# A new written-out order for a fused retention and channel-mix kernel

## The chip, the cores and the metric

The kernel runs on one core of one Trainium2 chip. The metric is the device time of one execution in microseconds. The core has five engines with queues of their own: TensorE (PE, with its weight loads shown apart as PEld), VectorE (DVE), ScalarE (ACT), GpSimd (POOL) and SyncE (SP, which only issues DMAs here). Each engine works its own list in order and waits for the others through semaphores. Sixteen DMA engines move the data.

## The reference

The inputs q, k and v have the shape batch 4, heads 8, time 768, width 64. The first half is a recurrent attention with a decay gamma for each head; the second half is a channel mix on its result, with 512 channels and 1024 hidden ones:

```python
for t in range(S):
    state = gamma * state + einsum('bhd,bhe->bhde', k[:, :, t], v[:, :, t])
    y[:, :, t] = scale * einsum('bhd,bhde->bhe', q[:, :, t], state)
x = y.transpose(0, 2, 1, 3).reshape(B, S, H * D)
x_prev = x shifted by one step in time, zero at the start
xk = mu_k * x + (1 - mu_k) * x_prev
xr = mu_r * x + (1 - mu_r) * x_prev
k = relu(xk @ w_k)
out = sigmoid(xr @ w_r) * (k * k @ w_v)
```

## The kernel before

The sequence of each batch is cut into three blocks of 256 steps, so there are 12 blocks, 0 to 11; a state is carried through the three blocks of one batch. Within a block the recurrence is done as matrix products: masked scores inside two chunks of 128 steps (u = 0 and 1), and a state T32 or TG that is decayed from chunk to chunk.

The whole program is one long list of words, the text ORDER at line 16, written out by hand or by a planner; the loop at the end of the kernel takes word after word and calls the function of its code. A word's code is what is done, its first number the block, and the numbers behind @ are the banks of the accumulator memory (PSUM, eight banks, 0 to 7) that it writes. The order of the words is the order of each engine's list. Tiles are used in rings, so a piece also waits until the last reader of its ring slot is done: four slots for q, k and v each, three for scaled keys, turned q and k, masked scores, mixed inputs and hidden values, two for differences, five for gates and results.

| code | line | engine | what |
|---|---|---|---|
| lq, lv, wk, wv, wr | 176, 511, 518, 514 | GpSimd's DMA queue | load q, v (cast to 16 bits), halves of w_k and w_v, w_r |
| lk | 176 | SyncE's queue, or GpSimd's where its third place is 2 | load k |
| ks | 189 | VectorE (last number 0) or GpSimd (1) | scale the keys by their decay |
| T, Tq, Tk | 204, 222 | TensorE | turn keys or q (T in 128 x 128 pieces, Tq and Tk in 64 x 64) |
| E | 250 | ScalarE | copy turned q (0) or k (1) from PSUM |
| S, M | 258, 265 | TensorE, VectorE | scores; mask them |
| C, U, G | 283, 295 or 299, 302 | TensorE, VectorE, GpSimd | state of a block; add; decay |
| I, Y, D | 314, 327, 341 | TensorE, TensorE, VectorE | output from the state; from the masked scores; to xT |
| Du, du, Xu, Ku, Qu | 349, 356, 370, 387, 395 | | block 0's D, dx, X, K and Q in halves of 128 steps |
| dx, X | 356, 370 | VectorE or GpSimd; VectorE | difference to the step before; mixed inputs, four slices for each of xk (0) and xr (1) |
| K, Q | 407, 414 and 417 | TensorE, ScalarE | a quarter of the hidden layer; relu and square |
| R, s | 421, 427 | TensorE, ScalarE | gate product; sigmoid |
| V, O, st | 433, 439, 446 | TensorE, VectorE, SyncE's queue | value product in two parts; result; store |
| Vc, Oc, sc | 451, 458, 466 | | the last half block's V, O and st in two halves |
| z | 495 | TensorE | zero matmuls, as many as the number says |
| mu, mt, me | 483, 488, 491 | ScalarE's queue, TensorE, ScalarE | load mu; turn it; copy it |
| gy | 501, 504 | VectorE | powers of the decay |

A word such as `lq.0.0.2` loads only the slices 0 to 2 of four: block 0's q and k come in halves. `Ku.0.1.0` is the second half of the hidden layer (1) for the first 128 steps (0) and reads the second half of w_k, `wk.1`. `V.n.tb.0` reads `wv.0` and the first half of the hidden values, `V.n.tb.1` the rest.

Two places of the code matter for the steps. A load's queue is chosen by the word, and a bank or ring slot is what ties pieces together beyond their data:

```python
def load_k(n, e=0, j0=0, j1=NJ):
    load((nc.sync, nc.scalar, nc.gpsimd)[e], k, K32, n, j0, j1)
def store(n, tb):
    nc.sync.dma_start(out=out[b, t0 : t0 + P, :], in_=OS(2 * n + tb))
```

Of the kernel before, what the change touches and what calls it, by code (L numbers as in the profile page):

```python
# [25 lines left out]
V.0.0.0@7 R.0.1@2 R.0.0@0 V.0.1.1 D.1 dx.1.0 X.1.0.1.2 X.1.0.2.3 X.1.0.3.4 X.1.0.0.1 s.0.0 s.0.1
X.1.1.0.1 O.0.1 X.1.1.1.2 ks.2.0 X.1.1.2.3 X.1.1.3.4 K.1.3@0 lq.4 lv.3 lq.5 Q.1.3 K.1.0@2 K.1.2@6
Tq.2@01 Q.1.0 E.2.0 C.2@2 T.2.1@4 E.2.1 V.0.0.1 R.1.0@0 Q.1.2 lv.5 U.1.1 G.1.1 U.2.0 G.2.0 ks.3.1
ks.4.1 O.0.0 S.2.0@45 M.2.0 I.2.0@67 S.2.1@23 K.1.1@1 R.1.1@4 T.3.1@5 s.1.0 Q.1.1 ks.5.1 M.2.1 Y.2
D.2 dx.2.0 Tq.3@23 V.1.1.0@1 V.1.1.1 T.4.1@0 T.5.1@6 V.1.0.0@7 E.3.0 s.1.1 E.3.1 E.4.1 O.1.1  # L30
S.3.0@01 Tq.4@45 V.1.0.1 E.5.1 E.4.0 X.2.0.1.2 X.2.0.2.3 M.3.0 X.2.0.0.1 X.2.0.3.4 C.3@23 S.4.0@45
Tq.5@01 U.3.0 X.2.1.2.3 X.2.1.0.1 U.3.1 M.4.0 E.5.0 K.2.2@6 K.2.1@2 K.2.3@3 Q.2.2 Q.2.1 I.3.0@45
S.3.1@01 lv.4 lk.6.2 lk.7.2 lq.6 G.3.1 lv.6 lq.7 X.2.1.1.2 X.2.1.3.4 M.3.1 O.1.0 ks.6.0 K.2.0@2
R.2.1@6 Q.2.3 Q.2.0 s.2.1 Y.3 S.5.0@23 C.4@01 D.3 V.2.1.0@6 T.6.1@7 R.2.0@4 V.2.1.1 V.2.0.0@5
V.2.0.1 E.6.1 s.2.0 lk.10 st.0.0 dx.3.1 M.5.0 X.3.0.0.1 X.3.0.2.3 X.3.0.1.2 X.3.0.3.4 X.3.1.2.3
K.3.1@4 K.3.0@7 U.4.0 G.4.0 O.2.0 U.4.1 O.2.1 ks.7.1 G.4.1 Q.3.1 Q.3.0 I.4.0@45 Tq.6@01 S.4.1@23
K.3.2@6 K.3.3@7 M.4.1 X.3.1.0.1 X.3.1.3.4 X.3.1.1.2 C.5@2 Y.4 U.5.0 st.1.0 lk.9 st.2.0 lk.11
# [538 lines left out]
```

## Time and profile before

| what | value |
|---|---|
| median of 3 runs | 160.04 us (159.6, 160.04, 162.05) |
| the profiled execution | 160.76 us |
| its span, first to last instruction | 158.7 us |
| busy: PE, DVE, ACT, POOL | 149.2, 123.6, 93.8, 63.4 us |
| read from and written to memory | 24.25 MB, 6.29 MB |
| first half of q, v, second half of q of block 0 landed | 6.65, 8.09, 8.81 us |
| v, k and q of block 1 landed | 11.28, 12.81, 14.08 us |
| wk.0, wk.1, wv.0, wr, wv.1 landed | 16.60, 19.13, 21.69, 24.23, 26.77 us |
| q, k and v of block 2, k of block 3 landed | 28.27, 30.15, 31.30, 33.14 us |
| first Ku, first V, Y.4 started | 18.20, 23.42, 61.33 us |

The profile is one execution. Its page gives the busy time of each engine, a chain that leads from the last instruction back to what released each step, and groups of instructions by line. Times count from the start of the span; the execution's own time is 2.1 us longer than its span. Landings are the times at which the trace shows a load complete. A busy PE is one with a matmul under way, and its ends are modelled. Steps between the starts of pieces are used where pieces overlap a little.

### The profile page before, as it was taken

How to read it: one execution, taken by the hardware profiler on the slowest of the kernel's cores; microseconds unless marked ns; L12 is line 12 of the kernel's file. 1: busy time of each engine (PE TensorE's matmuls, PEld its weight loads, DVE VectorE, ACT ScalarE, POOL GpSimd, SP SyncE). 2: the span in 40 equal slices, each digit the busy share in tenths (PEclk: the TensorE clock that was granted, in tenths of full speed). 3: DMA queues.
4: the chain of work that ended last, by engine and by line, in shares of the span. 5: the costliest groups of instructions: out<-in, count | busy, mean ns of one | idle time of the engine just before them, and what ended most of it. 6: DMA issues, size and time to landing. Idle time of an engine off the chain costs nothing.

```text
span 158.7 us, 5766 instructions
## 1 busy us (share of the span) xinstructions
PE 149.2 (94%) x2564; PEld 96.6 (61%) x2564; DVE 123.6 (78%) x217; ACT 93.8 (59%) x149; POOL 63.4 (40%) x69
## 2 busy tenths in 40 slices
PE   6977899899998999998999999999999999999991
PEld 2344683766585577575667576576486585675760
DVE  2568899776998789999969789975997887992321
ACT  3230665775977349467667675277665556276950
POOL 7937593589932457703013306291014114000000
PEclk9999999999999999999999999999999999999999
DMA  5999999999999986999408910712050050001242
GB/s 149 168 243 207 208 206 246 281 260 185 136 287 164 235 268 163 290 179 131 45 10 321 126 14 4 68 46 95 0 202 0 0 202 4 0 0 66 82 172 80
DMA packets 36872, 21.99 MB, mean 139 GB/s; under 512 B 25832, under 2 KB 32880, under 8 KB 36848
## 3 DMA queue, kind: packets, MB, share of 16 engines
q0 software_dynamic: 28768, 13.11, 59.2%
q1 hardware_dynamic: 7632, 8.26, 15.3%
q8 instruction: 20, 0.33, 0.8%
q10 hardware_dynamic: 448, 0.26, 0.6%
q14 instruction: 4, 0.03, 0.1%
HBM read 24.25 MB, written 6.29 MB: 192 GB/s over the span
## 4 chain that ended last, share of the span: by engine, by line
PE 79%; DMA 10%; DVE 4%; POOL 2%; issue 2%; DVEq 0%; POOLq 0%
PE ps L433 24%; PE ps L407 23%; PE ps L421 12%; DMA k<-in_k_dram 7%; PE ps L258 4%; DMA q<-in_q_dram 4%; PE ps L327 4%; PE ps L314 3%; PE ps L222 3%; PE ps L283 2%; PE ps L204 2%; POOL q L176 1%; PE ps L451 1%; DVE xk L370 1%; PE ps L495 1%
## 5 line engine op out<-in xcount | busy, mean ns | idle before, releaser
L433 PE MATMUL ps<-wv,k 128*128 128x512 f16 x184 | 44.9, 380 | 0.0
L407 PE MATMUL ps<-xk,wk 128*128 128x256 f16 x352 | 43.2, 273 | 0.0
L414 ACT ACTIVATE kr<-ps 128x512 f32<-128x512 f32 x44 | 26.0, 591 | 21.9 <-PE ps L407 21.9
L407 PEld LDWEIGHTS <-wk 128*128 128x128 f16 x352 | 33.2, 98 | 8.1 <-DVE xk L370 0.7
L265 DVE TENSOR_TENSOR a<-ps,c_sb 128x1024 f16<-128x1024 f32 (+1 forms) x26 | 29.2, 1137 | 2.3 <-PE ps L258 2.3
L417 ACT ACTIVATE k<-kr 128x512 f16<-128x512 f32 x44 | 27.7, 630 | 1.4
L433 PEld LDWEIGHTS <-k 128*128 128x128 f16 x184 | 17.1, 98 | 18.3 <-ACT k L417 1.0
L302 POOL TENSOR_TENSOR tg<-t,csm_sb 128x256 f16<-128x256 f32 x16 | 9.8, 610 | 43.9 <-DVE t L299 43.9
L421 PE MATMUL ps<-wr,xr 128*128 128x512 f16 x96 | 24.4, 379 | 0.7 <-issue 0.7
L439 DVE SCALAR_TENSOR_TENSOR os<-ps,rs 128x512 f32<-128x512 f32 x23 | 15.5, 686 | 11.6 <-ACT rs L427 8.4
L370 DVE SCALAR_TENSOR_TENSOR xk<-dx,mu,xT 128x256 f16<-128x256 f32 (+1 forms) x52 | 21.4, 459 | 2.9 <-POOL dx L356 2.7
L370 DVE SCALAR_TENSOR_TENSOR xr<-dx,mu,xT 128x256 f16<-128x256 f32 (+1 forms) x52 | 21.9, 459 | 0.0
L427 ACT ACTIVATE rs<-ps 128x512 f32<-128x512 f32 x24 | 13.8, 592 | 12.1 <-PE ps L421 12.1
L250 ACT COPY kT<-ps 128x1024 f16<-128x1024 f16 (+1 forms) x13 | 12.1, 953 | 11.1 <-PE ps L204 7.7
L341 DVE TENSOR_TENSOR xT<-ps,gy_sb 128x1024 f32<-128x1024 f32 x11 | 13.4, 1223 | 5.3 <-PE ps L327 3.8
L250 ACT COPY qT<-ps 128x1024 f16<-128x1024 f16 (+1 forms) x13 | 12.2, 940 | 8.6 <-PE ps L222 7.8
L421 PEld LDWEIGHTS <-xr 128*128 128x128 f16 x96 | 8.9, 98 | 10.3 <-issue 1.1
L176 POOL DMA_DIRECT2D v<-in_v_dram x12 | 10.8, 904 | 10.3 <-PE ps L327 4.7
L189 POOL TENSOR_TENSOR ks<-k,csm_sb 128x1024 f16<-128x1024 f32 x7 | 13.2, 1899 | 2.5 <-DMA k<-in_k_dram 2.5
L176 POOL DMA_DIRECT2D q<-in_q_dram x13 | 11.7, 898 | 3.3 <-PE ps L421 1.6
L258 PE MATMUL ps<-qT,kT 64*64 64x128 f16 x384 | 11.9, 220 | 1.1 <-ACT qT L250 0.7
L356 POOL TENSOR_TENSOR dx<-xT 128x1024 f32<-128x1024 f32 x4 | 7.6, 1891 | 9.1 <-DVE xT L341 9.1
(45 smaller groups left out, 144.5 us busy)
## 6 DMA issues: line engine op xcount, KB each, us to landing
out_dram<-os SPq DMA_DIRECT2D x23, 256.0 KB, 2.6
k<-in_k_dram POOLq DMA_DIRECT2D x8, 512.0 KB, 9.4
v<-in_v_dram POOLq DMA_DIRECT2D x12, 256.0 KB, 6.1
q<-in_q_dram POOLq DMA_DIRECT2D x11, 256.0 KB, 8.3
k<-in_k_dram SPq DMA_DIRECT2D x3, 512.0 KB, 5.2
wk<-in_moe_w_k_dram POOLq DMA_DIRECT2D x2, 512.0 KB, 11.1
wv<-in_moe_w_v_dram POOLq DMA_DIRECT2D x2, 512.0 KB, 12.5
k<-in_k_dram SPq DMA_DIRECT2D x2, 256.0 KB, 3.6
```

The costliest lines, as they stand in the source:

```text
L176: eng.dma_start(out=d(n)[:, 2 * j0 : 2 * j1], in_=rows(x, n)[:, 2 * j0 : 2 * j1])
L250: nc.scalar.copy(out=out, in_=pt)
L258: nc.tensor.matmul(pa[u * D : u * D + D, hp, j, :], lhsT=KT(n)[r, j, i, u * D : u * D + D], rhs=QT(n)[r, j, u, :], start=(j == j0), stop=( ...
L265: nc.vector.tensor_tensor(out=A2(n)[:, i, :, j0:j1], in0=pairs(banks("S", n, i, j0))[:, :, j0:j1], in1=causal[:, i, None, None, :].to_broa ...
L370: nc.vector.scalar_tensor_tensor(out=XM[w](n)[:, j, t0:t1], in0=DX(n)[:, j, t0:t1], scalar=mu[:, w * NCO + j : w * NCO + j + 1], in1=x[:, ...
L407: nc.tensor.matmul(pz[:, i, :], lhsT=wk16[:, co, fo * P : fo * P + P], rhs=XM[0](n)[:, co, :], start=(i == 0 and co == 0), stop=(co == NCO ...
L414: nc.scalar.activation(out=kr, in_=banks("K", n, g).rearrange("p (i t) -> p i t", i=2), func=AF.Relu)
L417: nc.scalar.activation(out=K2(n)[:, 2 * g : 2 * g + 2], in_=kr, func=AF.Square)
L421: nc.tensor.matmul(banks("R", n, tb), lhsT=XM[1](n)[:, co, tb * P : tb * P + P], rhs=wr16[:, co, :], start=(co == 0), stop=(co == NCO - 1),)
L427: nc.scalar.activation(out=RS(2 * n + tb), in_=banks("R", n, tb), func=AF.Sigmoid, scale=1.0 / KSC)
L433: nc.tensor.matmul(banks("V", n, tb, 0), lhsT=K2(n)[:, fo, tb * P : tb * P + P], rhs=wv16[:, fo, :], start=(fo == 0), stop=(fo == NFO - 1),)
L439: nc.vector.scalar_tensor_tensor(out=OS(2 * n + tb), in0=banks("V", n, tb, 0), scalar=1.0 / (KSC * KSC), in1=RS(2 * n + tb), op0=ALU.mult, ...
```

## The change

Only the text ORDER is changed. The same pieces of work are put in another order, with these differences in kind:

- v of block 0 is loaded ahead of both halves of q; v of block 1 comes behind wk.1, wk.1 ahead of wk.0, and k and q of block 2 ahead of wr, wv.0 and wv.1.
- k of block 10 goes to GpSimd's queue; blocks 9 and 11 stay on SyncE's, among other stores.
- The keys of blocks 1, 3, 4 and 5 are scaled on VectorE instead of GpSimd, those of 2, 6, 8 and 9 on GpSimd instead of VectorE.
- The differences of blocks 3, 7, 9 and 10 are on VectorE instead of GpSimd, those of 4, 5, 6 and 8 on GpSimd instead of VectorE.
- The keys of blocks 5 and 9 are turned in 64 x 64 pieces and those of 8 in 128 x 128; before, 8 was in 64 x 64 pieces and 5 and 9 were not.
- There are 24 zero matmuls instead of 27, and the load of mu is issued behind the first copy of ScalarE.
- Many banks are given out anew.

```diff
-lk.0.0.2.4 lk.0.0.0.2 lq.0.0.2 lv.0 lq.0.2.4 lv.1 lk.1.2 mu gy ks.0.0.2.4 ks.0.0.0.2 z.13@2
-Tq.0.0.2@01 lq.1 wk.0 wk.1 T.0.1.0.2@2 T.0.1.2.4@3 E.0.0.0.2 E.0.1.0.2 z.2@4 C.0@01 U.0.0 U.0.1
-wv.0 G.0.1 ks.1.1 wr wv.1 Tq.0.2.4@45 S.0.0.0.2@67 E.0.0.2.4 E.0.1.2.4 z.2@2 I.0.0@45 S.0.1.0.2@01
-S.0.0.2.4@23 M.0.0.0.2 M.0.0.2.4 mt@6 M.0.1.0.2 z.1@7 S.0.1.2.4@23 M.0.1.2.4 z.3@7 Y.0 z.2@7
-C.1@23 Du.0.0 Du.0.1 me T.1.1@4 Tq.1@01 E.1.1 E.1.0 z.4@7 S.1.0@01 du.0.0.0 du.0.0.1 Xu.0.0.0.2.3
-Xu.0.0.1.2.3 Xu.0.0.1.3.4 Xu.0.0.1.1.2 Xu.0.0.1.0.1 Ku.0.0.1@4 Xu.0.0.0.1.2 U.1.0 G.1.0 lq.2
-lk.2.2 M.1.0 Xu.0.1.0.2.3 Xu.0.0.0.3.4 Xu.0.0.0.0.1 Ku.0.1.1@2 Qu.0.0.1 lv.2 I.1.0@45 S.1.1@01
-lk.3.2 lk.4.2 lq.3 lk.5.2 Ku.0.1.0@6 Ku.0.0.0@7 Qu.0.1.0 Qu.0.0.0 Qu.0.1.1 Xu.0.1.0.1.2
-Xu.0.1.1.1.2 M.1.1 Y.1 Xu.0.1.0.3.4 Xu.0.1.1.2.3 Xu.0.1.1.3.4 Xu.0.1.0.0.1 Xu.0.1.1.0.1 V.0.1.0@6
-V.0.0.0@7 R.0.1@2 R.0.0@0 V.0.1.1 D.1 dx.1.0 X.1.0.1.2 X.1.0.2.3 X.1.0.3.4 X.1.0.0.1 s.0.0 s.0.1
-X.1.1.0.1 O.0.1 X.1.1.1.2 ks.2.0 X.1.1.2.3 X.1.1.3.4 K.1.3@0 lq.4 lv.3 lq.5 Q.1.3 K.1.0@2 K.1.2@6
-Tq.2@01 Q.1.0 E.2.0 C.2@2 T.2.1@4 E.2.1 V.0.0.1 R.1.0@0 Q.1.2 lv.5 U.1.1 G.1.1 U.2.0 G.2.0 ks.3.1
-ks.4.1 O.0.0 S.2.0@45 M.2.0 I.2.0@67 S.2.1@23 K.1.1@1 R.1.1@4 T.3.1@5 s.1.0 Q.1.1 ks.5.1 M.2.1 Y.2
-D.2 dx.2.0 Tq.3@23 V.1.1.0@1 V.1.1.1 T.4.1@0 T.5.1@6 V.1.0.0@7 E.3.0 s.1.1 E.3.1 E.4.1 O.1.1
-S.3.0@01 Tq.4@45 V.1.0.1 E.5.1 E.4.0 X.2.0.1.2 X.2.0.2.3 M.3.0 X.2.0.0.1 X.2.0.3.4 C.3@23 S.4.0@45
-Tq.5@01 U.3.0 X.2.1.2.3 X.2.1.0.1 U.3.1 M.4.0 E.5.0 K.2.2@6 K.2.1@2 K.2.3@3 Q.2.2 Q.2.1 I.3.0@45
-S.3.1@01 lv.4 lk.6.2 lk.7.2 lq.6 G.3.1 lv.6 lq.7 X.2.1.1.2 X.2.1.3.4 M.3.1 O.1.0 ks.6.0 K.2.0@2
-R.2.1@6 Q.2.3 Q.2.0 s.2.1 Y.3 S.5.0@23 C.4@01 D.3 V.2.1.0@6 T.6.1@7 R.2.0@4 V.2.1.1 V.2.0.0@5
-V.2.0.1 E.6.1 s.2.0 lk.10 st.0.0 dx.3.1 M.5.0 X.3.0.0.1 X.3.0.2.3 X.3.0.1.2 X.3.0.3.4 X.3.1.2.3
-K.3.1@4 K.3.0@7 U.4.0 G.4.0 O.2.0 U.4.1 O.2.1 ks.7.1 G.4.1 Q.3.1 Q.3.0 I.4.0@45 Tq.6@01 S.4.1@23
-K.3.2@6 K.3.3@7 M.4.1 X.3.1.0.1 X.3.1.3.4 X.3.1.1.2 C.5@2 Y.4 U.5.0 st.1.0 lk.9 st.2.0 lk.11
-st.0.1 st.1.1 lk.8.2 G.5.0 lq.8 Q.3.2 E.6.0 Q.3.3 V.3.1.0@6 R.3.1@0 V.3.1.1 s.3.1 D.4 dx.4.0
...
-Q.11.0 K.11.2@5 Q.11.2 K.11.3@1 O.9.0 X.11.1.0.1 Q.11.3 V.11.0.0@0 R.11.0@5 V.11.0.1 R.11.1@1
-Vc.11.1.0@4 Vc.11.1.1@6 s.11.0 st.8.1 st.7.1 st.8.0 O.10.1 O.10.0 st.9.0 st.10.1 st.10.0 st.9.1
-O.11.0 st.11.0 s.11.1 Oc.11.1.0 Oc.11.1.1 sc.11.1.0.0 sc.11.1.1.1
+lk.0.0.2.4 lk.0.0.0.2 lv.0 lq.0.0.2 lq.0.2.4 gy lk.1.2 lq.1 ks.0.0.2.4 wk.1 lv.1 ks.0.0.0.2 z.12@1
+T.0.1.0.2@0 T.0.1.2.4@1 E.0.1.0.2 mu z.5@4 Tq.0.0.2@23 C.0@45 E.0.0.0.2 Tq.0.2.4@67 U.0.0
+E.0.0.2.4 S.0.0.0.2@23 U.0.1 E.0.1.2.4 M.0.0.0.2 I.0.0@67 G.0.1 S.0.1.0.2@45 S.0.1.2.4@01
+M.0.1.0.2 wk.0 S.0.0.2.4@23 M.0.0.2.4 lk.2.2 M.0.1.2.4 lq.2 ks.1.0 Y.0 Tq.1@01 wr Du.0.0 mt@2 wv.0
+Du.0.1 T.1.1@6 me E.1.0 du.0.0.0 lv.2 du.0.0.1 E.1.1 wv.1 Xu.0.0.0.0.1 Xu.0.1.0.1.2 Xu.0.1.0.3.4
+lk.3.2 Xu.0.0.0.2.3 z.3@4 S.1.0@67 C.1@01 Xu.0.1.0.2.3 Xu.0.0.0.3.4 Xu.0.0.1.0.1 Xu.0.0.1.3.4
+Xu.0.0.0.1.2 Xu.0.1.1.0.1 Xu.0.0.1.2.3 z.4@4 Ku.0.1.0@2 Xu.0.1.1.1.2 Xu.0.0.1.1.2 Xu.0.1.1.3.4
+Ku.0.0.0@3 Xu.0.1.0.0.1 Qu.0.1.0 U.1.0 M.1.0 G.1.0 Ku.0.0.1@0 Qu.0.0.0 I.1.0@45 Xu.0.1.1.2.3
+S.1.1@23 U.1.1 Qu.0.0.1 Ku.0.1.1@6 M.1.1 G.1.1 ks.2.1 Tq.2@01 Qu.0.1.1 Y.1 R.0.0@6 D.1 lq.3
+R.0.1@7 s.0.0 lq.4 dx.1.0 E.2.0 T.2.1@6 lv.3 V.0.0.0@4 E.2.1 X.1.0.0.1 lq.5 X.1.0.1.2 V.0.1.0@5
+X.1.0.3.4 s.0.1 X.1.0.2.3 lk.4.2 S.2.0@01 X.1.1.1.2 C.2@7 M.2.0 K.1.2@6 lk.5.2 K.1.1@2 X.1.1.2.3
+X.1.1.3.4 X.1.1.0.1 K.1.3@3 Q.1.1 U.2.0 G.2.0 V.0.1.1 Q.1.2 lk.6.2 I.2.0@01 S.2.1@67 Q.1.3 K.1.0@2
+M.2.1 V.0.0.1 O.0.1 R.1.1@3 O.0.0 ks.3.0 st.0.0 Y.2 s.1.1 Tq.3@45 Q.1.0 D.2 R.1.0@3 lq.7 E.3.0
+V.1.1.0@2 lk.7.2 dx.2.0 s.1.0 V.1.1.1 lq.6 X.2.0.0.1 Tq.4@45 lv.4 X.2.0.3.4 C.3@01 X.2.0.1.2 E.4.0
+Tq.5@67 X.2.1.0.1 lv.6 V.1.0.0@3 X.2.0.2.3 E.5.0 X.2.1.1.2 V.1.0.1 U.3.0 ks.4.0 T.3.1@0 K.2.0@6
+O.1.1 E.3.1 ks.5.0 K.2.1@7 Q.2.0 K.2.2@0 O.1.0 Q.2.1 U.3.1 I.3.0@45 S.3.1@67 G.3.1 S.3.0@23 Q.2.2
+M.3.1 T.4.1@1 ks.6.1 V.2.0.0@0 E.4.1 M.3.0 K.2.3@6 lk.8.2 X.2.1.3.4 Y.3 Q.2.3 X.2.1.2.3 Tk.5@23
+lv.5 D.3 R.2.1@1 V.2.1.0@6 dx.3.0 s.2.1 E.5.1 V.2.1.1 X.3.1.2.3 X.3.1.0.1 V.2.0.1 O.2.1 Tq.6@23
+X.3.0.3.4 st.2.1 S.4.0@67 X.3.1.1.2 E.6.0 C.4@45 st.0.1 X.3.0.0.1 lk.9 R.2.0@1 X.3.0.1.2 st.1.0
+X.3.0.2.3 T.6.1@2 X.3.1.3.4 s.2.0 K.3.2@3 U.4.0 E.6.1 O.2.0 G.4.0 K.3.0@4 M.4.0 lv.7 Q.3.2 K.3.3@2
+U.4.1 Q.3.0 G.4.1 I.4.0@67 C.5@3 S.4.1@45 Q.3.3 ks.7.1 U.5.0 R.3.1@0 M.4.1 K.3.1@1 s.3.1 G.5.0
+lk.11 Y.4 Q.3.1 ks.8.1 I.5.0@45 S.5.0@01 D.4 R.3.0@2 st.2.0 M.5.0 st.1.1 V.3.0.0@3 dx.4.1 s.3.0
+S.5.1@67 Tk.7@01 M.5.1 T.8.1@2 lk.10.2 V.3.0.1 E.8.1 X.4.0.2.3 X.4.0.1.2 lq.8 V.3.1.0@6 E.7.1
+O.3.0 V.3.1.1 lv.8 X.4.0.0.1 lq.10 Tq.7@01 O.3.1 S.6.0@23 E.7.0 Y.5 X.4.0.3.4 C.6@67 D.5 K.4.1@0
...
+Q.8.1 X.9.0.1.2 S.10.0@01 C.10@23 X.9.0.2.3 C.11@7 Q.8.2 M.10.0 V.7.0.0@4 Q.8.0 V.7.0.1 U.10.0
...
+R.9.1@5 D.11 s.9.0 K.9.2@1 s.9.1 dx.11.0 V.9.0.0@0 Q.9.2 K.10.2@1 X.11.0.0.1 O.8.0 K.10.1@5
...
+X.11.1.1.2 R.10.1@0 st.9.1 Q.11.2 K.11.0@1 K.10.3@7 R.10.0@6 Q.10.3 R.11.0@7 s.10.0 V.10.1.0@5
+s.11.0 K.11.1@4 K.11.3@7 Q.11.1 V.10.0.0@4 Q.11.0 V.10.0.1 Q.11.3 V.10.1.1 O.10.0 s.10.1
+V.11.0.0@7 st.10.0 O.10.1 V.11.0.1 st.10.1 R.11.1@6 O.11.0 Vc.11.1.0@5 st.11.0 s.11.1 Vc.11.1.1@4
+Oc.11.1.0 sc.11.1.0.0 Oc.11.1.1 sc.11.1.1.1
```

## The prediction

> **What bounds the kernel now.** I read the page's busy shares first, then the chain that ended last, the waits, the stages, and last the timeline of the first 20 us.
>
> ```profile
> PE 149.2 (94%) x2564; PEld 96.6 (61%) x2564; DVE 123.6 (78%) x217; ACT 93.8 (59%) x149; POOL 63.4 (40%) x69
> ...
> 18.20:35.00 16.80, 16.34 (x283) 11.32 (x276) 14.36 (x28) 11.50 (x19) 11.80 (x15) 1.00 1.33 243
> 35.00:60.00 25.00, 24.21 (x509) 16.68 (x502) 21.44 (x32) 16.30 (x25) 15.67 (x14) 1.00 1.27 210
> ...
> 100.00:155.20 55.20, 55.18 (x762) 35.55 (x748) 39.81 (x68) 33.74 (x56) 10.56 (x10) 1.00 0.23 68
> 155.20:158.70 3.50, 0.00 (x0) 0.00 (x0) 0.42 (x1) 0.00 (x0) 0.00 (x0) 1.00 0.22 75
> ```
>
> The columns of a stage are its length, then PE, PEld, DVE, ACT, POOL. TensorE is the bound: from 18.2 us on it is idle for about 1.7 us in 137 before its last matmul ends at 155.2. An order can gain only where TensorE waits: the head (its first 18.2 us), single waits, and the last 3.5 us.
>
> ```profile
> 3.07 5.74 DMA q<-in_q_dram
> ...
> 14.66 0.73 DVE dx L356 x2
> ...
> 50.19 0.79 issue
> ...
> 73.95 0.72 issue
> ```
>
> In the chain (start, length, what) the reader sees the head wait for the second half of q of block 0, then for VectorE. Two stalls of 0.8 and 0.7 us have no releaser; I take them to recur.
>
> ```profile
> 12.88 1.90 POOL L189 TENSOR_TENSOR ks<-k,csm_sb 128x1024 f16<-128x1024 f32 x1 [2.53 <-DMA k<-in_k_dram]
> 17.85 0.42 PE L258 MATMUL ps<-qT,kT 64*64 64x128 f16 x16 [0.67 <-ACT qT L250]
> 18.20 2.04 PE L387 MATMUL ps<-xk,wk 128*128 128x128 f16 x32
> ```
>
> Block 1's keys are scaled on GpSimd until 14.78; their turn and copies follow, S.1.0 starts at 17.85 and the first Ku at 18.20.
>
> **The change, part by part.** Removed, added and moved pieces have the same durations (steps from start to start, of one engine's busy stretches): on TensorE K 0.88, V and R 0.865, Ku 0.95, T 0.47, Tq and Tk 0.33; on VectorE M 1.14, D 1.15, dx 1.2, X 0.40, Xu 0.26, U 0.36, O 0.61, ks 1.15; on ScalarE Q 1.16, E 0.93. GpSimd keeps seven ks and four dx. One full turn (T) becomes a small one (Tk): 0.1 less. Three zero matmuls less fill waits only: nothing.
>
> Loads of block 0. The halves of q landed at 6.65 and 8.81, v at 8.09; the second half took 0.72 behind v. All three carry the same bytes, so with v first they land near 7.4, 8.1 and 8.8. The last stays. The first half of q is 1.4 later: its turn goes from 6.70 to 8.1, under five zero matmuls, and C.0 from 8.13 to 8.4, so U.0.0 and U.0.1 end at 9.7 rather than 9.66. Moving v alone is worth 0, bounded by -0.1 and +0.3.
>
> Masks of block 0. VectorE idled 0.53 us before M.0.0.2.4 at 10.78. With the second mask taken first that gap closes: the four masks end near 12.3, not 12.67.
>
> ks.1 goes from GpSimd to VectorE, ahead of Du.0.0, and waits for k of block 1; Du, du and every Xu queue behind it. In the load queue k of block 1 takes the place of v of block 1, which landed 2.47 after q; its own interval was 1.53. It lands at 10.3 to 11.3, under the masks. ks ends at 13.5 and Y.0 at 13.1, so Du starts at 13.5 (13.37 before). Two Du and two du (0.61, 0.68) end at 16.05.
>
> The first Ku now stands behind nine Xu instead of five: 16.05 + 9 x 0.26 = 18.4, so 18.5 against 18.20: **+0.3**. The old gate is gone: S.1.0 can go at 15.9, C.1 when v of block 1 lands (16.5). Three Ku, I.1, S.1.1 and the fourth Ku end at 22.9. Y.1 needs M.1.1, behind fifteen Xu (19.95), U.1.0, M.1.0, one Xu and U.1.1: it ends at 23.2, so Y.1 starts at 23.3 against 22.63, with Tq.2 (0.3) already done.
>
> Weights. Loads of GpSimd's queue landed one behind the other: 2.53 us for half of wk, 2.54 for wr or half of wv, 1.88 for k, 1.50 for q. From k of block 1 at 11.3: q 1.27, half wk 2.53, v 1.45, half wk 2.53, k 1.88, q 1.50, wr 2.54 make 25.0, and wv.0 27.55. In the trace a ninth load of this queue was issued half a microsecond after the first of the eight before it had landed (k of block 5 at 24.77, wr at 24.23); here that keeps the queue full. TensorE ends Y.1 at 23.9 and now waits for wr until 25.0 (bounds 24.0 and 26.0, by k's interval and an extra microsecond). Queued behind R.0.0 is all of TensorE. R twice, T.2.1: 27.2; V waits for wv.0: 27.55. Two V, S.2.0, C.2, three K, V.0.1.1, I.2, S.2.1, K.1.0 and V.0.0.1 end at 35.65. Before, V.0.0.1 ended at 33.14, and S.2.0, I.2.0, S.2.1 and K.1.1, which come earlier now, took 34.10 to 36.00: 35.04 for the same work. **The head costs +0.6**, bounded by -0.5 and +1.6.
>
> From 35.65 to Y.4 TensorE has 8 K, 8 V, 5 R, 3 T, 5 Tq or Tk and small pieces: 25.1 us. Waits that the order holds: V.1.1.0 for Q.1.0 0.3, S.3.1 and V.2.0.0 for a bank each 0.2, one unexplained stall 0.8. Y.4 then starts at 62.2 (61.33 before) with 0.4 more work done: **+0.5**. The bounds of what I can't see are nothing and 2 us.
>
> Behind Y.4 I look at what each TensorE piece needs and how much TensorE work lies between. Waits over 0.5 us don't stand out (K.10.2 behind Q.9.2, C.11 behind Q.8.1, some 0.6 to 0.8, before partly taken up by queued work). Before had the like. The moves of k cost nothing: SyncE sends k of blocks 9 and 11 near 55 and 62, needed near 87 and 91; k of block 10, now on GpSimd's queue near 66, is needed near 103. New is st.2.1 ahead of st.0.1 on SyncE: it waits until 53.7, and O.3.0, which needs the buffer, comes at 66. The end is alike: two Vc, a multiply of 0.42, a store.
>
> One DMA is moved under load: mu is issued at about 7.6 instead of 1.72, behind the first copy. mu is needed by the first Xu at 16.1. SyncE's k of block 10, issued amid GpSimd's loads, landed in 5.2; 7.6 + 0.9 + 5.2 is 13.7. It is hidden.
>
> [...]
>
> **Sum.** The profiled execution took 160.76 with a span of 158.7, so 161.3 by its own time. It lies 0.7 above the median of 160.04; moved to the median: **160.6**.
>
> **Rivals.** *VectorE becomes the bound from 35 to 62 (slower).* It takes over ks.3, ks.4 and ks.5 there. Its work from O.0.1 to M.4.1: 3 ks 3.45, 2 D 2.3, 2 dx 2.4, 16 X 6.4, 5 U 1.8, 4 M 4.56, 6 O 3.66: 24.6 us against TensorE's 25.1, where the stage above had 21.44 against 24.21. It starts at 35.0, waits some 1.2 us for inputs, and has about 1.4 us to spare. In it ks.4 and ks.5 wait at 42.5 and 44.2 for keys that land near 40.4 and 42.0 by the same sums. For it: 38 pieces, each of which loses up to 0.08 of overlap when it waits, make 3 us, and a dx once took 1.52. Against it: ks and X held their durations beside a busy GpSimd. It decides once VectorE or the keys are over 1.4 to 2 us later than summed; at 4 to 6 us later it costs 2.5 to 4.5: 163 to 165. Chance 0.22.
>
> *The head gains (faster).* If k, wk and wr land a microsecond earlier (1.53 for k) R.0.0 doesn't wait, and if the unexplained stalls stay out (1.5) the sum is 160.6 - 1.0 - 1.5 = 158.1; over 2% takes one more microsecond, from waits of 0.4 and 0.9 near 31 and 14 us that are gone without others in their place. Chance 0.18.
>
> *The change doesn't do what it says.* v first is hidden by the second half of q: then only the rest of the order counts, which is my forecast.
>
> **How the numbers follow.** Forecast 159 to 162.3: 0.60. Rival above: 0.22, of which 0.20 lies over 163.2. Faster rival: 0.18, of which 0.05 lies under 156.8. 2% (3.2 us) is about what a measurement of this kernel can tell from no change. So faster 0.05, within 0.75, slower 0.20. The range leaves out the ends of both rivals: 157.4 to 164.6.
>
> **What would show it.** Tq.0.0.2 at 8.1 and Tq.0.2.4 at 8.8; ks.1 on VectorE ending near 13.5; first Ku near 18.5; a wait for wr of about 1 us before R.0.0 near 24; Y.4 near 62; TensorE over 94% busy and its end near 155.7. The prediction is wrong if VectorE shows no idle time from 35 to 62 and TensorE waits for masks or mixes there, or if any load's landing ends a TensorE wait of over 1.5 us.

## The result and the profile after

The changed kernel took 162.05 us in the median of four runs (161.48 to 166.89), the kernel before 159.82 in the same comparison (158.91 to 162.05). The ratio is 1.0114 with a 95% interval from 1.0066 to 1.0162: some 1.8 us slower, inside the 2% that the forecast allowed for and in the upper half of its range. The ratio leaves out the run of 166.89 us, which had the lowest granted clock (0.959). The profiled execution took 161.48 us with a span of 159.4; before it was 160.76 with 158.7.

The page of the changed kernel: busy time of each engine, and the granted clock in 40 slices of the span.

```profile
PE 148.8 (93%) x2585; PEld 97.4 (61%) x2585; DVE 122.5 (77%) x217; ACT 93.3 (59%) x149; POOL 64.1 (40%) x70
...
PEclk9999599999999999999999999999999999999999
...
q8 instruction: 20, 0.33, 0.8%
```

TensorE has 21 matmuls more than before (24 more since one full turn of keys, of 8, became small ones, of 32; three zeros less) and is busy for a similar time. The fifth slice shows half the clock, which the kernel before did not have. The last line is a queue that neither the order nor the forecast speaks of: 20 packets, 0.33 MB, of kind "instruction". Much of what follows hangs on it.

The stages, with the columns of the forecast (start and end, length, then PE, PEld, DVE, ACT, POOL, the clock, DMA share, GB/s):

```profile
18.20:35.00 16.80, 16.70 (x282) 11.96 (x281) 14.09 (x29) 10.70 (x18) 9.87 (x11) 0.96 1.46 215
35.00:60.00 25.00, 24.25 (x492) 15.95 (x492) 23.45 (x37) 17.39 (x26) 10.14 (x11) 1.00 1.18 224
...
100.00:155.20 55.20, 55.12 (x756) 36.02 (x754) 39.48 (x67) 34.64 (x58) 6.17 (x6) 1.00 0.18 67
155.20:159.40 4.20, 0.58 (x6) 0.27 (x3) 0.65 (x2) 0.00 (x0) 0.00 (x0) 0.99 0.25 85
```

VectorE carries 23.45 of 25 us from 35 to 60, two more than before, and TensorE is still busy for 24.25 of them. The matmuls end at 155.78 instead of 155.18: the profiled loss is in the head and in the middle, and nothing is lost behind.

The chain that ended last (start, length, what):

```profile
2.31 6.70 DMA q<-in_q_dram
...
14.66 12.61 DMA wv<-in_moe_w_v_dram
27.31 1.90 PE ps L433 x8
...
43.20 0.28 PE ps L204 x5
43.48 0.75 issue
44.22 0.33 PE ps L204 x3
...
74.20 0.89 issue
```

The head now ends with wv.0, as the forecast had it. The two stalls without a releaser are there again, 0.75 and 0.89 us, but the first has moved: it cuts T.3.1 into five and three matmuls.

The timeline of VectorE and TensorE in the head:

```profile
13.29 1.21 DVE L189 TENSOR_TENSOR ks<-k,csm_sb 128x1024 f16<-128x1024 f32 x1
...
16.86 0.64 PE L258 MATMUL ps<-qT,kT 64*64 64x128 f16 x16 [0.18 <-ACT kT L250]
17.29 0.64 PE L283 MATMUL ps<-v,ks 64*64 64x64 f16 x32
17.86 1.78 PE L495 MATMUL ps<-zero 128*128 128x512 f16 x4
19.48 2.84 PE L387 MATMUL ps<-xk,wk 128*128 128x128 f16 x48
...
24.87 1.90 PE L421 MATMUL ps<-wr,xr 128*128 128x512 f16 x8
26.61 0.61 PE L204 MATMUL ps<-c_sb,ks 128*128 128x128 f16 x8
27.31 1.04 PE L433 MATMUL ps<-wv,k 128*128 128x512 f16 x4
```

ks.1 ends at 14.50 and the first Ku starts at 19.48, each a microsecond behind the forecast; R.0.0 follows Y.1 without a wait, and the first V starts 0.04 us behind the landing of wv.0 (27.27).

### The profile page after: what moved, and what is told of

Same layout as the page of the kernel before. It is cut to its first block, busy times and chain, and to the rows that moved or that the text cites. A ratio compares the mean times of both kernels' runs of the same rounds, so it can differ in the third digit from the quotient of the medians.

```text
span 159.4 us, 5799 instructions
## 1 busy us (share of the span) xinstructions
PE 148.8 (93%) x2585; PEld 97.4 (61%) x2585; DVE 122.5 (77%) x217; ACT 93.3 (59%) x149; POOL 64.1 (40%) x70
## 3 DMA queue, kind: packets, MB, share of 16 engines
HBM read 24.25 MB, written 6.29 MB: 192 GB/s over the span
## 4 chain that ended last, share of the span: by engine, by line
PE 77%; DMA 12%; POOL 3%; ACT 3%; issue 2%; DVE 1%; DVEq 0%; POOLq 0%
PE ps L433 26%; PE ps L407 22%; PE ps L421 12%; DMA wv<-in_moe_w_v_dram 8%; DMA q<-in_q_dram 4%; PE ps L258 3%; PE ps L314 3%; PE ps L327 3%; PE ps L222 3%; PE ps L283 2%; PE ps L204 1%; ACT kr L414 1%; ACT k L417 1%; PE ps L451 1%; POOL v L176 1%
## 5 line engine op out<-in xcount | busy, mean ns | idle before, releaser
L433 PE MATMUL ps<-wv,k 128*128 128x512 f16 x184 | 44.0, 379 | 0.1
L407 PE MATMUL ps<-xk,wk 128*128 128x256 f16 x352 | 42.6, 273 | 0.0
L407 PEld LDWEIGHTS <-wk 128*128 128x128 f16 x352 | 33.7, 98 | 7.5 <-issue 0.2
L433 PEld LDWEIGHTS <-k 128*128 128x128 f16 x184 | 17.2, 98 | 18.2 <-ACT k L417 0.3
L302 POOL TENSOR_TENSOR tg<-t,csm_sb 128x256 f16<-128x256 f32 x16 | 9.8, 610 | 40.4 <-DVE t L299 40.4
L421 PE MATMUL ps<-wr,xr 128*128 128x512 f16 x96 | 23.9, 380 | 0.0
L370 DVE SCALAR_TENSOR_TENSOR xk<-dx,mu,xT 128x256 f16<-128x256 f32 (+1 forms) x52 | 21.9, 456 | 0.1
L258 PE MATMUL ps<-qT,kT 64*64 64x128 f16 x384 | 11.3, 224 | 0.2 <-ACT kT L250 0.2
```

The lines of the kernel that those rows point to most:

```text
L258: nc.tensor.matmul(pa[u * D : u * D + D, hp, j, :], lhsT=KT(n)[r, j, i, u * D : u * D + D], rhs=QT(n)[r, j, u, :], start=(j == j0), stop=( ...
L370: nc.vector.scalar_tensor_tensor(out=XM[w](n)[:, j, t0:t1], in0=DX(n)[:, j, t0:t1], scalar=mu[:, w * NCO + j : w * NCO + j + 1], in1=x[:, ...
L407: nc.tensor.matmul(pz[:, i, :], lhsT=wk16[:, co, fo * P : fo * P + P], rhs=XM[0](n)[:, co, :], start=(i == 0 and co == 0), stop=(co == NCO ...
L421: nc.tensor.matmul(banks("R", n, tb), lhsT=XM[1](n)[:, co, tb * P : tb * P + P], rhs=wr16[:, co, :], start=(co == 0), stop=(co == NCO - 1),)
L433: nc.tensor.matmul(banks("V", n, tb, 0), lhsT=K2(n)[:, fo, tb * P : tb * P + P], rhs=wv16[:, fo, :], start=(fo == 0), stop=(fo == NFO - 1),)
```

## The head: who gates the first V

**v of block 0 back between the halves of q, in the changed kernel:**

```diff
-lk.0.0.2.4 lk.0.0.0.2 lv.0 lq.0.0.2 lq.0.2.4 gy lk.1.2
+lk.0.0.2.4 lk.0.0.0.2 lq.0.0.2 lv.0 lq.0.2.4 gy lk.1.2
```

> The kernel after, with v of block 0 put back between the two halves of q; k of block 1 still goes directly behind the second half. In the profile after, that half landed at 9.87 us (8.81 before), while the 4096-byte packets of k of block 1 were already moving (from about 7.0 us). Theory one, the neighbour: the load that stands directly ahead of k of block 1 is held up by it, whatever the order of q and v. Then the first half of q lands near 6.7, v near 8.3, and the second half still near 9.8; the first Ku stays at 19.4 to 19.5 and the first V at 27.2 to 27.4, the span at 159 to 159.8. Theory two, v first is what delays: the second half lands near 8.8 and the first Ku starts near 18.4.

The halves of q landed at 6.21 and 8.39, v at 7.63; with v first the changed kernel had 8.30 (v), 9.02 and 9.87. That doesn't decide between the two theories, since this landing varies by nearly as much with the order of the loads unchanged (below). The first Ku came at 18.93 and the first V at 26.51, behind wv.0 at 26.25; the granted clock was half from 12.12 to 18.94. A single run took 161.1 us, with stalls of 0.85 and 1.16 us.

**v first alone, in the kernel before:**

```diff
-lk.0.0.2.4 lk.0.0.0.2 lq.0.0.2 lv.0 lq.0.2.4 lv.1
+lk.0.0.2.4 lk.0.0.0.2 lv.0 lq.0.0.2 lq.0.2.4 lv.1
```

> The kernel before with one part of the change alone: v of block 0 ahead of both halves of q. The zeros stay. By my forecast's step (all three carry the same bytes) the second half of q lands at 8.8 and nothing changes: within 0.3 us. By the landings since, it comes 0.3 to 1 us later, near 9.1 to 9.8; the first masks, Y.0 and Du move with it, but S.1.0 and the first Ku hang on the keys of block 1 on GpSimd (ended at 14.78), so the first Ku starts at 18.2 to 18.5 and the time rises by 0 to 0.4 us. The clock stays whole.

Measured: 160.65 us, ratio 1.0043 (1.0008 to 1.0078). The loads landed at 7.47, 8.19 and 8.92, close to the forecast of 7.4, 8.1 and 8.8. Yet the first Ku came at 19.3 instead of 18.20 and the first V at 24.47 instead of 23.42. TensorE's timeline has the first turn of q in the kernel before, then the same turn, two zeros and C.0 in this run:

```profile
6.70 0.32 PE L222 MATMUL ps<-c_sb,q 64*64 64x64 f16 x16 [0.36 <-DMA q<-in_q_dram]
...
8.23 0.32 PE L221 MATMUL ps<-c_sb,q 64*64 64x64 f16 x16 [1.89 <-DMA q<-in_q_dram]
...
8.94 0.95 PE L494 MATMUL ps<-zero 128*128 128x512 f16 x2
9.83 0.64 PE L282 MATMUL ps<-v,ks 64*64 64x64 f16 x32
```

In this order the turn of q stands ahead of the turn of the keys, two zeros and C.0, so all of them wait with it: TensorE is idle for 1.89 us instead of 0.36, and C.0 comes at 9.83 instead of 8.13. The granted clock was half from 9.04 to 12.45 us, where the kernel before had it whole, and made it longer (two zeros took 0.95 us, 0.59 before). So in this order v first has a price of its own, 0.1 to 1.2 us, from the idle time and the clock together; how much each is worth is not shown. In the changed order the turns of the keys and five zeros stand ahead of that turn, so the price need not be the same there.

**q of block 1 ahead of k of block 1:**

```diff
-gy lk.1.2 lq.1 ks.0.0.2.4
+gy lq.1 lk.1.2 ks.0.0.2.4
```

> The kernel after, with q of block 1 loaded ahead of k of block 1, so that q of block 1 stands directly ahead of k. Theory one, the neighbour: the second half of q of block 0 lands near 8.8 instead of 9.87, and q of block 1 takes its place near 12 to 12.5; k of block 1 lands near 12.7 instead of 11.4, so the scaling of its keys on VectorE waits and ends near 14.0 instead of 14.50, and the first Ku starts near 19.0 instead of 19.48. Theory two, v first: the second half of q stays near 9.8 and the first Ku comes later than 19.5. On the span: the weights wv.0 land at 27.3 in either order, and the first V started 0.04 behind them; if TensorE's path and the weights are two gates at one level, the half microsecond doesn't come out and the time is that of the kernel after within 0.3 us. If TensorE's path alone sets the head, it is 0.5 us shorter.

162.12 us, ratio 1.0087 (1.0050 to 1.0124). The first Ku came at 18.65, 0.8 earlier, and all of it was lost again: R.0.0 waited 0.73 us for wr (25.27) and V started at 27.84 behind wv.0 (27.80).

**No load of wr.** The weights of the gate are zero here; the gate's matmuls are done on them, and the load is left out.

```diff
-Tq.1@01 wr Du.0.0 mt@2 wv.0
+Tq.1@01 Du.0.0 mt@2 wv.0
...
+        nc.vector.memset(wr16, 0.0)
```

> The kernel after without the load of the gate's weights: the tile is set to zero on VectorE in the first microseconds, so the gate is one half everywhere; this part of the computation is left out. GpSimd's queue has 1 MB less to move ahead of wv.0. Theory two gates at one level: wv.0 lands 2.5 us earlier, near 24.8, but TensorE reaches the first V only behind Y.1, two R and T.2.1, as after: it starts at 27.2 instead of 27.31, and the span falls by 0.1 to 0.3. Theory weights alone: the first V starts about 2 us earlier and the span falls by as much.

wv.0 landed at 24.50, 2.8 us earlier, and V still started at 27.44. The timeline of TensorE in this run:

```profile
19.51 3.21 PE L386 MATMUL ps<-xk,wk 128*128 128x128 f16 x48
...
25.26 1.90 PE L420 MATMUL ps<-wr,xr 128*128 128x512 f16 x8
27.00 0.61 PE L203 MATMUL ps<-c_sb,ks 128*128 128x128 f16 x8
27.44 1.89 PE L432 MATMUL ps<-wv,k 128*128 128x512 f16 x8
```

From R.0.0 to V TensorE does not wait once. So two gates stand near the same level: the queue of weights (27.27 in the changed kernel) and TensorE's own path (27.1 by the starts of its pieces there, 27.44 here, where the granted clock was half from 13.43 to 20.26 us, twice as long). Taking away one of them alone gives at most some 0.3 us at V, which is what the last two runs show from both sides. The single run without wr took 160.22 us all the same: its matmuls ended at 154.52, 1.26 earlier than in the changed kernel, though V came no earlier. Its unexplained stalls came to 0.44 us instead of 1.64, which is nearly all of that.

## The zeros, and a theory that fell

Because the clock fell in the changed kernel's head, I added zero matmuls to its gaps: six ahead of T.1.1, then 19 in all, then the 19 with v back between the halves.

```diff
-Du.0.1 T.1.1@6
+Du.0.1 z.6@4 T.1.1@6
```

> The kernel after, with six more zero matmuls between the turn of q and the turn of k of block 1, where TensorE idled for 0.9 us. In the profile after, the granted clock was half from 16.00 to 19.41 us, and over the runs the times follow the mean granted clock: 161.48 at 0.989, 162.34 at 0.977, 166.89 at 0.959. Theory clock: low activity in the head costs clock windows, in some runs more than one; with the zeros the clock stays whole in the profile and in most runs, the first Ku starts near 19.35, the median falls by 0.3 to 1 us and the runs lie closer together. Theory no clock: the zeros only fill a wait; clock and times stay as they were, within 0.3 us in the median.

161.91 us, ratio 1.0103 (1.0065 to 1.0141): nothing gained, and the granted clock was still half in its profile, from 13.12 to 16.53. The second half of q landed at 9.01 in this run and at 9.87 in the changed kernel's, with the loads in the same order; the other runs of that order have 8.67 to 9.32. So a microsecond of such a landing is scatter. The stall near 43.5 was gone (0.03), and in its place there were 0.32 and 0.48 us near 24 and 30.

```diff
-I.0.0@67
+z.2@0 I.0.0@67
...
-Y.0 Tq.1@01
+z.6@4 Y.0 Tq.1@01
...
-T.1.1@6
+z.7@4 T.1.1@6
...
-z.4@4 Ku.0.1.0@2
+z.8@4 Ku.0.1.0@2
```

> The kernel after with zero matmuls in all the gaps of its head: 2 ahead of I.0.0, 6 ahead of Y.0, 7 ahead of T.1.1, and 8 instead of 4 ahead of the first Ku. Runs of the kernel after and of its variants had a mean granted clock of 0.96 to 1.0, and their traces show half clock for one or two stretches of 3.4 us between 12 and 20 us; all runs of the kernel before were at 0.995 to 1.0. Six zeros in one place did not hold it. Theory clock: TensorE is too little busy between 8 and 16 us in the new order, since its zeros stand elsewhere; with zeros in every gap the clock stays at 0.995 to 1.0 in all runs, and the median falls from 162.05 to 161 or less, with a narrower spread. Theory no cost: the clock may come back, but half clock falls on zeros and waits alone (z.4 ended 0.3 us behind its Xu), so the median stays at 161.5 to 162.3.

165.5 us, ratio 1.0324 (1.0273 to 1.0375): some 3.4 us slower than the changed kernel, though the clock was whole in the head and V at 27.69 only 0.4 later. Both theories of the expectation fell. The timeline of TensorE around 42 us:

```profile
41.25 0.42 PE L221 MATMUL ps<-c_sb,q 64*64 64x64 f16 x26
44.14 0.25 PE L221 MATMUL ps<-c_sb,q 64*64 64x64 f16 x6 [2.47 <-issue]
```

TensorE stops for 2.47 us inside Tq.5, after 26 of its 32 matmuls. Tq.5 waits for nothing there, and no zero stands near it. From 45.3 to 48.7 the granted clock was half.

```diff
-lv.0 lq.0.0.2 lq.0.2.4
+lq.0.0.2 lv.0 lq.0.2.4
```

> The kernel after with the zeros in its gaps as in the run beside it, and v of block 0 back between the halves of q. In four runs with v first the second half of q landed at 9.01 to 9.87 us, in two with v between at 8.39 and 8.81. Theory two gates at one level: the second half lands at 8.4 to 8.9, the first Ku starts 0.5 to 0.9 us earlier, near 18.7, but the first V still waits for wv.0 near 27, so the time is at most 0.3 us below that of the run beside it. Theory v first: the time falls by 0.5 to 0.9 us.

164.7 us, ratio 1.0300 (1.0245 to 1.0355), with the first V at 27.18 behind wv.0 (27.13) and a stall of 2.77 us in the same Tq.5. That is 0.8 us under the run above, as "Theory v first" had it, but the two intervals overlap over most of their length, so it decides nothing. The other direction is the kernel before without ten of its zeros:

```diff
-z.2@4 C.0@01
+C.0@01
...
-z.2@2 I.0.0@45
+I.0.0@45
...
-z.1@7 S.0.1.2.4@23 M.0.1.2.4 z.3@7 Y.0 z.2@7
+S.0.1.2.4@23 M.0.1.2.4 Y.0
```

> The kernel before without the ten zero matmuls that stand between the first turns and S.1.0 (2, 2, 1, 3 and 2); the 13 at the start and the 4 ahead of S.1.0 stay. Theory clock: the granted clock now drops in the head of the kernel before too, to 0.96 to 0.99, with half clock somewhere between 10 and 20 us, and the median rises by 0.5 to 2 us. Theory no clock: the zeros only filled waits; clock whole, time within 0.3 us of the kernel before, or a little less.

160.09 us, ratio 1.0008 (0.9978 to 1.0038). The granted clock was half from 13.79 to 17.20, and yet the profiled execution took 158.81, the fastest of twelve, its matmuls ending at 153.24: both stalls were gone, none over 0.2 us was left behind 40 us. All twelve had a mean granted clock of 0.958 to 0.989, under that of nearly every run of the kernel before, and the median is the same. Either the lower clock cost nothing there, or the stalls that went paid for it; the run doesn't tell which.

## What the stalls are

Counted from 0 in order of time, matmuls, weight loads and TensorE's few waits of its own together, the stalls of over 0.3 us that no other engine and no load ends are, in all these runs, just ahead of TensorE's instruction 1473, 1729, 2753 or 3521 (705 and 961 in the run with six zeros more): the distances are multiples of 256. The instruction queue moves 20 packets of 16,384 bytes in the span, one for about each 256 of TensorE's instructions (5,139 before, 5,179 in the changed kernel). I read this as TensorE's program coming in pieces of 256, with the next piece not there yet at a stall; what a packet holds no trace shows. Times in us, out of the traces; the packet is the one of the piece that TensorE stops for:

| run | piece begins | used up | packet starts | TensorE goes on |
|---|---|---|---|---|
| before | 43.80 | 50.19 | 48.66 | 50.98 |
| before | 69.99 | 73.95 | 72.36 | 74.67 |
| changed | 37.45 | 43.48 | 41.73 | 44.22 |
| changed | 69.65 | 74.20 | 72.84 | 75.09 |
| 19 zeros more | 37.67 | 41.67 | 41.71 | 44.14 |

TensorE goes on 2.2 to 2.6 us after the packet starts, in all 28 such stalls of the study. In the traces of before and after a packet starts 0.8 to 4.9 us behind the beginning of the piece ahead of it, as long as loads run (to 80 us); later 2.2 us ahead of it to 1.6 behind. By this reading a piece must last some 6.5 us near 40 us (an estimate: 4.0 to 4.3 us in the two rows that begin near 37.5, and 2.4). A piece with many short matmuls (Tq, C: 64 instructions in about 0.3 to 0.45 us) doesn't: the one of the last row was used up in 4.00.

If the program comes in such pieces, instructions alone must be able to make the stall, without work. **The changed kernel with 19 short zero matmuls:**

```diff
+    def tiny(count):
+        for _ in range(count):
+            nc.tensor.matmul(
+                banks("zt", count)[:, 0:64], lhsT=zero[:, 0:P], rhs=zero[:, 0:64], start=True,
+                stop=True, skip_group_check=True,
+            )
-z.5@4 Tq.0.0.2@23
+z.5@4 zt.9@4 Tq.0.0.2@23
...
-T.1.1@6
+zt.10@4 T.1.1@6
```

> The changed kernel with 19 short matmuls on zeros added (64 columns each): nine ahead of the first transposes of q, ten ahead of the transposes of k of block 1. With their weight loads that is 38 TensorE instructions more, as many as the zeros in the gaps added, but hardly any work. Fetch theory: TensorE's program comes in pieces of 256 instructions; the next piece is asked for when one begins, and arrives some 6.4 us later where loads run (4.0 to 4.3 us until its packet starts, 2.4 from there). With 38 more instructions ahead, the piece that begins near 37.6 us holds all of the short transposes of blocks 4 and 5 and is used up in about 4 us: a stall of about 2.5 us near 41.7 in place of 0.75, and some 0.5 each at the ends of the pieces near 78 and 98. Sum 163.5 to 165.5 us. Rival, that the zeros cost by their time and what they do to the clock: 19 short matmuls are at most 0.3 us on the path, stalls stay at 0.75 and 0.89, 161.5 to 162.5 us.

165.56 us, ratio 1.0314 (1.0248 to 1.0379). The timeline of TensorE:

```profile
13.50 0.47 PE L501 MATMUL ps<-zero 128*128 128x64 f16 x10
...
24.81 1.90 PE L420 MATMUL ps<-wr,xr 128*128 128x512 f16 x8 [0.62 <-DMA wr<-in_moe_w_r_dram]
...
40.36 0.45 PE L221 MATMUL ps<-c_sb,q 64*64 64x64 f16 x32
40.63 0.44 PE L282 MATMUL ps<-v,ks 64*64 64x64 f16 x32
40.89 0.42 PE L221 MATMUL ps<-c_sb,q 64*64 64x64 f16 x26
43.95 0.25 PE L221 MATMUL ps<-c_sb,q 64*64 64x64 f16 x6 [2.64 <-issue]
...
78.63 0.21 PE L313 MATMUL ps<-qT,tg 64*64 64x128 f16 x1 [1.14 <-issue]
...
98.80 0.25 PE L221 MATMUL ps<-c_sb,q 64*64 64x64 f16 x6 [0.65 <-issue]
```

Ten of the short matmuls take 0.47 us in a gap, and the head is the one that was forecast: the second half of q at 8.79, the first Ku at 18.09, a wait of 0.62 us for wr until 24.8, V at 27.34 behind wv.0 (27.29). The stall is in Tq.5 after 26 matmuls, to the instruction where the full zeros had put it, and the two others are where the theory set them, the first of them larger (1.14 and 0.65 us, some 0.5 each expected). The loss adds up in the profiled execution: the matmuls end 4.6 us later than in the changed kernel, 2.8 of it more stall (4.43 against 1.64) and some 1.7 (an estimate: half of 3.41 us) from half the clock behind the long stall (44.74 to 48.15). The median is 3.5 us above the changed kernel's, just over the 163.5 to 165.5 expected. The rival, that zeros cost by their time, has at most 0.3 us. This and the run with the 19 full zeros are the largest effects of the study, here from 38 instructions that do nothing.

**Fewer instructions and the same busy time, in the kernel before and in the changed one:**

```diff
-    zero = const.tile([P, 512], F16, name="zero")
+    zero32 = const.tile([P, 512], F32, name="zero32")
+    zero = zero32.bitcast(F16)[:, 0:512]
...
-z.13@2
+zf.3@2 z.1@2
```

Here zf is the zero matmul on zero32. In the changed kernel z.12@1 becomes zf.3@1.

> The kernel before with twelve of the thirteen zero matmuls at the start replaced by three on zeros in f32: 18 TensorE instructions fewer, the other zeros all kept. How long one in f32 takes no run has shown; if it is about four of the others, TensorE stays busy up to the first transposes as before. Fetch theory: the ends of the pieces fall 18 instructions later in the order; by the times of the pieces in the trace of before and the same lateness of each fetch, the stalls near 50 and 74 (0.79 and 0.72 us) become 0.4 and 0; where 20 zeros' instructions had gone (the run with few zeros) none was left. So 0.8 to 1.5 us less: 158.3 to 159.2 us. Rival, that the stalls belong to the work at those places and not to the count: they stay, 159.8 us. If the clock falls in the head as it did with few zeros, the gain is lost again and about 160 us stand.

159.74 us against 159.99, ratio 0.9977 (0.9950 to 1.0005). The timeline of TensorE, with the zeros of the kernel before in the first line:

```profile
1.19 5.15 PE L495 MATMUL ps<-zero 128*128 128x512 f16 x13 [1.19 <-DVE xT L479]
...
1.45 5.32 PE L502 MATMUL ps<-zero 128*128 128x512 f32 x6 [1.45 <-DVE xT L479]
...
50.31 0.41 PE L327 MATMUL ps<-a,v 64*64 64x128 f16 x13 [0.36 <-issue]
```

Each zero in f32 shows as two matmuls, so 12 instructions went, not 18; the six lasted 5.32 us, the thirteen of before 5.15 (so a zero in f32 took some 1.77 us, and one in f16 0.40). The clock stayed whole. The stall near 50 is 0.36, the one near 74 is gone, and the profiled execution took 159.31 with its matmuls ending at 153.69, 1.5 earlier than before. The median gained only 0.25 us, where 0.8 to 1.5 were expected, and its interval includes no gain. So the count moved the stalls in the trace as the theory had it, and the size at the median missed. A likely reason, not shown, is that the profiled execution of before, on which the sum was made, lies 0.8 us above the median of its kernel (160.76 against 160.0), so that a usual run would have less to win.

> The same edit in the changed kernel: its twelve zeros at the start become three in f32, 18 instructions fewer. Fetch theory: here a shift by 18 trades one stall for others. By the pieces' times in its trace the stall near 43.5 goes from 0.75 to about 0.5, one of about 0.4 comes near 50, the one near 74 stays at 0.9 to 1.1: no gain, 161.3 to 162.5 us, a ratio of 1.008 to 1.015 to the kernel before. Rival, that fewer instructions or wider zeros are better in themselves: as much gained as in the kernel before, 160.5 to 161 us.

161.67 us, ratio 1.0067 (1.0032 to 1.0102): no gain on the changed kernel's 1.0114 that the intervals could tell (they overlap). The time is in the range of the fetch theory, the ratio a little under its 1.008 to 1.015. The stalls of this run:

```profile
44.75 1.47 PE L407 MATMUL ps<-xk,wk 128*128 128x256 f16 x12 [0.37 <-issue]
...
75.46 0.26 PE L283 MATMUL ps<-v,ks 64*64 64x64 f16 x9 [1.16 <-issue]
```

The first is half as long, the second longer: 1.53 against 1.64 us. The third that was expected, near 50, did not come. No version of this study beats the kernel before by more than its interval.

## VectorE's room

The forecast's main rival was VectorE between 35 and 62 us. Two operations more there, with no instruction more for TensorE:

```diff
-ks.4.0 T.3.1@0
+ks.4.0 ks.4.0 ks.4.0 T.3.1@0
```

> The changed kernel with the scaling of k of block 4 on VectorE done three times in a row instead of once: two operations of about 1.15 us more, 2.3 us, between 42 and 47 us, with no TensorE instruction more. My forecast gave VectorE a spare of 1.4 us in the stretch from 35 to 62 us (its only idle time there in the trace is 1.2 us, ahead of the masking of block 3): the masked scores of block 4 then start about 1.0 us later than at 62.5, and the end moves by 0.5 to 1.1 us. The rival that VectorE bounds this stretch: the whole 2.3 us come out, at 64.8 and at the end. If VectorE's work there has more room than its idle time shows: 62.5 as now.

The timelines of VectorE and TensorE in this run:

```profile
42.60 3.73 DVE L188 TENSOR_TENSOR ks<-k,csm_sb 128x1024 f16<-128x1024 f32 x3
...
48.71 0.41 PE L257 MATMUL ps<-qT,kT 64*64 64x128 f16 x14 [1.18 <-DVE os L438]
```

Of 2.3 us put in, 1.18 came out, as a wait of the scores behind a late result (O). Y.4 came 1.07 later (63.6), the last matmul 1.0 later; the single run took 162.5 us. So VectorE had about 1.1 us of room: the forecast's 1.4 less 0.3. The change went almost to the edge there. The rival's place and point of decision fit, though it did not happen; its price of 2.5 to 4.5 us at a delay of 4 to 6 was not tried.

## The prediction, step by step

**What held.** TensorE bounds the kernel (from 18.2 us on the kernel before is idle for 2.0 us up to its last matmul by its stages, not 1.7), and the head and single waits decide. V at 27.55 and V.0.0.1's end at 35.65 were forecast; 27.31 and 35.64 were measured, so the head's +0.6 holds to 0.1. Y.4 came at 62.51 (62.2 forecast), TensorE's end at 155.78 (155.7), the same tail behind it. The landing of k of block 4 (40.27, forecast 40.4) and of block 5 (42.06, 42.0) held, mu was hidden (turned and copied by 14.5), and the moves of k of blocks 9, 10 and 11 cost nothing that a trace shows: behind the stall near 74 TensorE has no idle time over 0.1 us up to its last matmul.

**What held for another reason.** The wait of R.0.0 for wr was to be 1.1 us, with TensorE ready at 23.9. It was nothing: TensorE itself came at 24.87. The first Ku was a microsecond late (19.48, not 18.5), since the second half of q landed at 9.87 rather than 8.8, the masks ended at 13.37 rather than 12.3, and so ks.1, Du and nine Xu followed a microsecond later; the zeros ahead of the first Ku, at half the clock, held it for the last 0.2 us (the ninth Xu ended at 19.26). Both gates lie near 27.3, so the error in one was covered by the other, which is luck: the runs with q of block 1 first and without wr show that either gate alone holds V there. So several of the forecast's own signs failed in this trace: Tq.0.0.2 came at 9.06 (8.1 forecast) and Tq.0.2.4 at 9.91 (8.8), ks.1 and the first Ku a microsecond late, and no wait for wr was there. TensorE was busy for 93%, not over 94. In the run with the short zeros the loads and the clock were as forecast, and there the wait for wr is seen.

The stretch from V.0.0.1 to Y.4 came out by two errors that cancel as well. TensorE's work in it was summed as 25.1 us and took 26.12. The waits of 0.3, 0.2 and 0.2 us that the order was to hold are not in the trace: its only idle time over 0.1 us there is the stall of 0.75.

**The terms that were wrong.** "Moving v alone is worth 0, bounded by -0.1 and +0.3": alone in the kernel before it cost 0.4% (0.1 to 1.2 us). "All three carry the same bytes" is true of the sum alone (v is 256 KB, each half of q 128 KB), and the landings came as forecast. What the step left out, in that order, is the work that stands in TensorE's list behind the first turn of q, 1.89 us of idle time, and half the clock. In the changed order no run tells the price from nothing. "Three zero matmuls less fill waits only: nothing" costed only their time. The stalls lie at the same few instruction numbers (1473, 1729, 2753, 3521), so the count of instructions ahead of a place in the order decided which work they cut, and 38 instructions more were worth 3.5 us at the median. In the same way the full turn that becomes a small one was counted as 0.1 us less; it is 24 matmuls and 24 weight loads more. "Two stalls of 0.8 and 0.7 us have no releaser; I take them to recur": they did, 1.64 us against 1.51, but they are no fixed tax; they went with 20 instructions fewer in the kernel before.

**The size.** By the profiled executions the step from before to after is 0.72 us, and 0.5 was forecast. By the medians it is 1.1%, 1.8 us. The profiled execution of before lies 0.9 above its median (160.76 against 159.82), that of the changed kernel 0.6 below its own (161.48 against 162.05). The forecast moved its sum to the median by the first of these and could not know the second. The runs without a profile don't show their stalls. Their mean granted clock was 0.959 to 0.989 in the changed kernel against 0.995 to 1.0 in all but one of the 58 listed runs of before, and v first alone shows much of that loss of clock (0.989 in most runs) with a third of the time; the run with few zeros lost as much of the clock and no time. What the rest is made of stays open; stalls that are longer in most runs than in the profiled one (1.98 and 2.01 us in the traces with q of block 1 first and with v between, against 1.64) would fit and were not isolated.

Also open is why a packet starts late. It goes with the loads in the traces of before and after (0.8 to 4.9 us behind the beginning of the piece ahead up to 80 us, 1.6 at most after that), but no run took all of them away. That a piece is asked for when the one ahead of it begins was a part of the theory that no trace shows; behind 80 us packets started up to 2.2 us before that. The nearest is the run without wr, which reads 1 MB less: the packet that started 4.3 us behind its piece in the changed kernel started 2.4 behind there, and the stall near 43.5 was gone. One trace doesn't show that the missing load did it.

## What to carry to other kernels

When a matmul stream stalls with no releaser, count instructions: if the stalls lie multiples of 256 apart and a packet of the instruction queue starts shortly ahead of their ends (2.2 to 2.6 us here), try an edit ahead of them that changes the count. Here 38 instructions more with hardly any work moved the stall from T.3.1 into Tq.5 (0.75 us to 2.64). The long stalls (2.47, 2.64 and 2.77 us) came where many short matmuls fell into one piece while loads ran; spreading them out was not tried. Before a sum is made against one profiled execution, see where that execution stands among the runs of its kernel, and look for a second gate at the same level before a wait is counted as a gain.

## What was not expected of the hardware

- The instruction queue moved 20 packets of 16,384 bytes in the span, one for about each 256 instructions of TensorE, and the stalls that nothing else ends lie multiples of 256 instructions apart. While loads ran, a packet started up to 4.9 us behind the beginning of the piece ahead, and at a stall TensorE went on 2.2 to 2.6 us after its start. The longest stall was 2.77 us, in the run with 19 zeros more and v between.
- The granted clock drops in stretches of 3.41 us or twice that (16.00 to 19.41 in the changed kernel, 13.43 to 20.26 in the run without wr). A stall of 2.47 and one of 2.64 us were followed by such a stretch (45.3 to 48.7, 44.74 to 48.15), one of 2.77 was not; the stretch then costs some 1.7 us more (an estimate: half of its 3.41).
- A zero matmul on f32 shows as two matmuls of 0.89 us each at the start, against 0.40 in f16 (5.32 us for six, 5.15 for thirteen).
